# Second-stage scores over all 128 rows from copied operands, and value products only behind the first stage's groups

## The chip, the cores and the metric

The kernel runs on one core of one Trainium2 chip. The metric is device time in microseconds of one execution. A core has TensorE (PE: matrix products and transposes through the PE; its weight loads are PEld in the profile), VectorE (DVE), ScalarE (ACT), GpSimd (POOL) and SyncE (SP), whose queue issues nearly all DMAs here.

## The reference, cut to what matters

Two stages, one behind the other, on 8 batches of 576 rows. The first stage is attention with 8 heads of 64 in which scores below the row's maximum less `tau` are dropped; the second is causal attention by 4 experts, of which each row keeps the two with the largest gate.

```python
# first stage: q, k, v are (8, 8, 576, 64)
scores = scale * (q @ k.T)
scores = where(scores >= max(scores) - tau, scores, -1e9)
attn = softmax(scores)
x = (attn @ v) with the heads side by side        # (8, 576, 512)

# second stage
w = softmax over the top 2 of x @ w_gate          # w_gate is (512, 4)
for e in range(4):
    q, k, v = x @ wq[e], x @ wk[e], x @ wv[e]     # 64 columns each
    a = softmax(causal(scale * (q @ k.T)))
    out += w[e] * (a @ v @ wo[e])                 # wo[e] is (64, 512)
```

## The kernel before, in words

Numbers are split in two parts where the product needs it: a high part in the rounded fp32 type (`F32R`, one pass of PE) and the rest, the low part. A product of q and k is then hi·hi + hi·lo + lo·hi; the constant `HHL` lists these three.

**First stage.** A pair `n` of heads (4 pairs a batch, 32 in all) is worked on in five steps, one for each tile of rows (`TS`: the tail tile of 64 rows first, then four of 128). `prep` transposes q and k of the next pair, splits them into `hl`, and DMAs on SP's queue copy the parts into `qt` and `kt` so that the high and the low part lie above each other in 128 rows: two products then do what three did. `scores` does the scores, maximum, threshold, exponential and scaling of one tile; `transp` transposes the probabilities of the tile two steps earlier (`LAG_T`) into buffers `pt`; `attnv` multiplies them with the values, three tiles at the fifth step and two at the second step of the next pair.

**Second stage.** When a batch has all its heads, `begin` lists three pieces of filling work: the projections of q and k for experts 0 and 1 (`q0`: ep = 0), the values and gates of all experts (`v`), and the projections for experts 2 and 3 (`q1`). `project` writes a tile `q2` (and one for k) whose rows 0 to 63 are one expert and rows 64 to 127 the other, high and low part beside each other in the free dimension. `scores2` makes the scores of one tile of rows `t` for both experts of a pair: for the four 128-row tiles there are six products over 64 rows each (three of `HHL`, two experts, alternating between the upper and the lower half of the array), and a mask product for each expert. The width is (t + 1) · 128 columns, as keys beyond the tile are masked. The tail tile, t = 4, has its own form, over 128 rows, from `q2ds`. Then `scale2` (sum, gate weight), `transp2`, `attnv2` and `output` follow.

**The order.** The order on PE is written out by hand as a plan: `queued` (line 152) adds up a plan clock `pe[1]` from a price for each instruction and 190 ns for each change of the weights' shape. Lists hold what may come next: `proj`, `S2` (tiles to be scored), `T2` (scored, to be transposed, each with an earliest plan time), `A2` (transposed, to be multiplied with the values) and `O2` (outputs). Inside a step, `fill` takes filling work until a goal, and `tiled`, called in the second to fifth step of a pair (at s = 1 and 4 behind a group of `attnv`, at s = 2 and 3 without one), does up to two value tiles and then scores one tile. After the last pair, a loop of its own works off the last batch. `pr` sets the priority by which the scheduler of the language orders instructions on each engine, SP's queue included.

Of the kernel before, what the change touches and what calls it, by code (L numbers as in the profile page):

```python
# [29 lines left out]
BETWEEN_S2, AFTER_V_END = 2000, 5000  # L30
# [9 lines left out]
T_END = (2, 3, 4, 1, 0)  # L40
# [15 lines left out]
PPB = 4  # L56
# [3 lines left out]
VB = 3  # L60
# [4 lines left out]
def kernel(  # L65
# [112 lines left out]
    def load_pair(n):  # L178
        b, hp = divmod(n, NPAIR)
        hs = slice(2 * hp, 2 * hp + 2)  # L180
        vm = one.tile([P, 2, R, D], F32, tag="vm", name=f"vm_{n}", bufs=VB)
        pr("ld")
        def load(dst, src):
            r = nc.sync.dma_start(dst, src)
            if n in (1, 2):
                tc.add_manual_dep(r.ins, SPREAD[0].name, NOSYNC, reason="order")
        for t, x in ((km, k), (qm, q)):
            load(t[:, :, :R], x[b, hs, :SM, :].rearrange("h (p r) d -> p h r d", r=R))
            load(t[:ST, :, R], x[b, hs, SM:, :].rearrange("h s d -> s h d"))
        load(vm, v[b, hs, :SM, :].rearrange("h (p r) d -> p h r d", r=R))  # L190
        for j, rows in enumerate((slice(0, ST), slice(ST, P))):
            load(vtz[n % VB][rows, j], v[b, 2 * hp + j, SM:, :])
        VS[n] = (vm, vtz[n % VB])

# [247 lines left out]
    q2ds = [zeros(f"q2d{i}") for i in range(2)]  # L442
    Q2, V2, GW, GT = {}, {}, {}, {}

    def project(b, ep, cs):

        first, last = cs[0] == 0, cs[-1] == NC - 1
        for i, (wh, wl) in enumerate(((wqh, wql), (wkh, wkl))):
            if last:
                Q2[b, ep, i] = one.tile([P, 2, S], F32R, tag=f"q2{ep}{i}", name=f"q2_{b}_{ep}_{i}")  # L450
# [89 lines left out]
    def scores2(b, t, ep):  # L540
        q2, k2 = Q2[b, ep, 0], Q2[b, ep, 1]
# [3 lines left out]
        if t < R:  # L545
            w = (t + 1) * P
# [5 lines left out]
            for i, (x, y) in enumerate(HHL):  # L552
                for j in range(2):
                    sl = slice(j * D, (j + 1) * D)
                    matmul(gg[j][:, :w], q2[sl, x, t * P:w], k2[sl, y, :w], start=(i == 0), stop=False)
            for j in range(2):
                matmul(gg[j][:, t * P:w], ident_b, mask, start=False, stop=True)
            views = [g[:, :w] for g in gg]
        else:
            w = S  # L560
            g = ps_s.tile([P, 2, 512], F32, tag="s", name=f"s2_{b}_{t}_{ep}")
            for hf in range(2):
                cols = slice(hf * HS, (hf + 1) * HS)
                for i, (x, y) in enumerate(HHL):
                    matmul(g[:, hf, :HS], q2ds[ep][:, x], k2[:, y, cols],
                                     start=(i == 0), stop=(hf == 0 and i == 2))
# [108 lines left out]
    def project_some():  # L675

        while proj:
            b, what, g = proj[0]
            if what == "v" and left.get(b - 1, 0) or any(x[1] == b - 1 and what == f"q{x[3]}" for x in S2):
                return False  # L680
            try:
# [4 lines left out]
                if what[0] == "q":  # L686
                    S2.extend((0, b, t, int(what[1])) for t in (T_MID if b < B - 1 else T_END))
                elif what == "v":
# [4 lines left out]

    def score_tile():
        _, b, t, ep = S2.pop(0)
        scores2(b, t, ep)
        if b in GW and not unscaled:
# [14 lines left out]
    def transposable():  # L712
        return due(T2) and len(unscaled) < len(T2) and len(A2) < 2
# [20 lines left out]
    def tiled():  # L734

        for _ in range(2):
            if due(A2):
                value_tile()
        if S2 and S2[0][2] < R and len(T2) < P2B:
            score_tile()  # L740
# [12 lines left out]
    load_pair(1)  # L753
    pre = iter(())
    goal = 0.0
    for i in range(N + 2):
# [24 lines left out]
        if slot:  # L781
            m, at = (n, 4) if s == 4 else (n - 1, 6)
            if 0 <= m < NPR:
                attnv(m, TS[slice(*AV_AT[at])])
                if at == 6 and m % NPAIR == NPAIR - 1:
                    begin(m // NPAIR)
            tiled()
        else:
            next(tr, None)
            if s in MORE:  # L790
                tiled()
# [10 lines left out]
        if S2 and S2[0][2] == R and len(T2) < P2B:  # L802
# [4 lines left out]
    while proj or S2 or T2 or A2 or O2:  # L807
# [9 lines left out]
        elif S2 and len(T2) < (P2B if S2[0][1] < B - 1 else PPB) and pe[1] >= since:  # L817
# [34 lines left out]
```

## Time and profile before

| what | number |
|---|---|
| median of 3 runs | 1035.93 us (1033.07 to 1035.97) |
| the profiled execution | 1033.38 us, span 1031.7 us |
| PE busy | 966.5 us, 94% of the span |
| DVE, ACT, POOL busy | 816.5, 651.6, 408.4 us |
| chain that ended last | PE 59%, DVE 17%, ACT 13%, issue 5%, POOL 4% |
| SP's queue, moved bytes | 83296 packets, 93.83 MB, 34.5% of 16 engines |

How to read it: a busy PE is not PE at its peak, because products are pipelined and overlap in the records; the distance from one start to the next says more. The chain is followed back from the last instruction, at each step to what released it. In rows of the timeline the columns are the start, the time to the end of the row's last instruction (us), the engine, the line of the code, the operation, the tiles as out<-in, the shape (rows * columns of the array, then the result), the number of instructions, and in brackets the idle time before it with what ended it. Line 159 is that of every matrix product and line 162 that of every transpose, since helpers issue them; tiles tell them apart. In rows of windows: the stretch, its length, and for each engine its busy time and its instructions, then the granted clock, the share of the DMA engines, and GB/s.

### The profile page before, as it was taken

How to read it: one execution, taken by the hardware profiler on the slowest of the kernel's cores; microseconds unless marked ns; L12 is line 12 of the kernel's file. 1: busy time of each engine (PE TensorE's matmuls, PEld its weight loads, DVE VectorE, ACT ScalarE, POOL GpSimd, SP SyncE). 2: the span in 40 equal slices, each digit the busy share in tenths (PEclk: the TensorE clock that was granted, in tenths of full speed). 3: DMA queues.
4: the chain of work that ended last, by engine and by line, in shares of the span. 5: the costliest groups of instructions: out<-in, count | busy, mean ns of one | idle time of the engine just before them, and what ended most of it. 6: DMA issues, size and time to landing. Idle time of an engine off the chain costs nothing.

```text
span 1031.7 us, 26572 instructions
## 1 busy us (share of the span) xinstructions
PE 966.5 (94%) x9520; PEld 863.5 (84%) x9520; DVE 816.5 (79%) x2374; ACT 651.6 (63%) x1564; POOL 408.4 (40%) x700
## 2 busy tenths in 40 slices
PE   4778999999999999999999999999999999999998
PEld 3676898789888898888987898978988889888975
DVE  4778688877888779888789878887788877988564
ACT  3667566765667656765667656676566765676554
POOL 2556424533244334443344332453324533433122
PEclk9998999999999999999999999999999999999999
DMA  6555423344223443225343242334322344311101
GB/s 156 142 128 141 121 73 91 102 117 119 59 72 95 133 112 93 61 68 143 90 103 94 72 124 75 91 102 126 110 56 73 96 132 112 79 30 44 42 2 46
DMA packets 83891, 96.11 MB, mean 93 GB/s; under 512 B 29745, under 2 KB 54321, under 8 KB 83761
## 3 DMA queue, kind: packets, MB, share of 16 engines
q1 hardware_dynamic: 83296, 93.83, 34.5%
q8 instruction: 76, 1.25, 0.5%
q10 hardware_dynamic: 464, 0.59, 0.2%
q14 instruction: 55, 0.44, 0.1%
HBM read 30.42 MB, written 9.44 MB: 39 GB/s over the span
## 4 chain that ended last, share of the span: by engine, by line
PE 59%; DVE 17%; ACT 13%; issue 5%; POOL 4%; DMA 1%; SPq 0%; DVEq 0%; ACTq 0%; POOLq 0%
PE av L159 18%; PE s L159 13%; PE tm L162 8%; PE pj L159 7%; DVE pp L356 5%; PE v L159 4%; PE o L159 4%; ACT p L575 3%; ACT pp L354 3%; PE t L162 3%; DVE nmx L349 3%; DVE x L439 2%; ACT pt L144 2%; PE qkT L162 2%; POOL pp L364 2%
## 5 line engine op out<-in xcount | busy, mean ns | idle before, releaser
L364 POOL TENSOR_SCALAR pp<-pp,ss 128x576 f32<-128x576 f32 x288 | 212.8, 750 | 408.4 <-DVE ss L370 313.0
L356 DVE SCALAR_TENSOR_TENSOR pp<-s,thr,pp 128x576 f32<-128x576 f32 x288 | 233.0, 814 | 77.3 <-ACT pp L354 72.5
L354 ACT ACTIVATE pp<-s,nmx 128x576 f32<-128x576 f32 x288 | 213.7, 746 | 80.6 <-DVE nmx L349 76.8
L349 DVE TENSOR_REDUCE nmx<-s 128x1 f32<-128x576 f32 x288 | 215.8, 751 | 41.6 <-PE s L159 40.4
L159 PE MATMUL s<-kt,qt 128*128 128x288 f32 x1024 | 205.3, 319 | 5.8 <-DMA qt<-hl 5.4
L162 PE MATMUL tm<-ident,pp 128*128 128x128 f32 x1152 | 166.2, 278 | 22.1 <-POOL pp L364 15.8
L159 PE MATMUL av<-pt,vm 128*64 128x128 f32 (+1 forms) x2560 | 167.8, 267 | 0.0
L159 PEld LDWEIGHTS s<-kt,qt 128*128 128x128 f32 x1024 | 151.9, 194 | 15.5 <-DMA qt<-hl 5.7
L162 PEld LDWEIGHTS tm<-ident,pp 128*128 128x128 f32 x1152 | 136.1, 143 | 33.2 <-POOL pp L364 22.6
L159 PEld LDWEIGHTS av<-pt,vm 128*64 128x64 f32 x2560 | 140.0, 138 | 15.4 <-issue 11.4
L144 ACT COPY pt<-tm 128x512 f32<-128x512 f32 x199 | 113.6, 589 | 58.6 <-PE tm L162 56.3
L575 ACT ACTIVATE p<-s,nm 128x384 f32<-128x384 f32 (+3 forms) x144 | 78.9, 551 | 63.4 <-DVE nm L573 59.0
L589 POOL TENSOR_SCALAR p<-p,sm,gw 128x512 f32<-128x512 f32 (+3 forms) x128 | 77.1, 610 | 81.4 <-ACT pt L144 35.4
L140 ACT ACTIVATE x<-av 128x256 fp32r<-128x256 f32 (+1 forms) x96 | 48.0, 500 | 71.5 <-PE av L159 49.6
L573 DVE TENSOR_REDUCE nm<-s 128x1 f32<-128x384 f32 (+3 forms) x144 | 71.1, 513 | 24.2 <-PE s L159 21.4
L162 PE MATMUL t<-ident,p 128*128 128x128 f32 x384 | 61.1, 284 | 15.9 <-DVE ss L369 8.9
L159 PE MATMUL av<-ptt,vtz 128*64 128x128 f32 (+1 forms) x640 | 68.8, 263 | 0.0
L140 ACT ACTIVATE pt<-t 128x512 f32<-128x512 f32 (+2 forms) x112 | 57.9, 541 | 15.6 <-PE t L162 14.2
L159 PE MATMUL v<-wvh,x 128*128 128x260 f32 x320 | 64.8, 287 | 0.0
L162 PEld LDWEIGHTS t<-ident,p 128*128 128x128 f32 x384 | 43.0, 144 | 25.9 <-POOL p L589 14.3
L439 DVE TENSOR_TENSOR x<-av,x 128x256 fp32r<-128x256 f32 (+1 forms) x96 | 47.6, 495 | 19.2 <-ACT x L140 16.0
L159 PE MATMUL av<-pt,v 128*64 128x128 f32 (+1 forms) x896 | 57.9, 262 | 1.9 <-ACT p L575 1.2
(132 smaller groups left out, 1808.9 us busy)
## 6 DMA issues: line engine op xcount, KB each, us to landing
kt<-hl SPq DMA_DIRECT2D x252, 144.0 KB, 2.7
qt<-hl SPq DMA_DIRECT2D x128, 128.0 KB, 2.4
km<-in_k_dram SPq DMA_DIRECT2D x32, 256.0 KB, 3.0
qm<-in_q_dram SPq DMA_DIRECT2D x32, 256.0 KB, 3.2
vm<-in_v_dram SPq DMA_DIRECT2D x32, 256.0 KB, 2.8
out_dram<-ob SPq DMA_DIRECT2D x32, 256.0 KB, 2.4
km<-in_k_dram SPq DMA_DIRECT2D x32, 32.0 KB, 2.7
qm<-in_q_dram SPq DMA_DIRECT2D x32, 32.0 KB, 2.7
```

Source lines behind the costliest of these rows:

```text
L140: nc.scalar.activation(dst, src, AF.Copy)
L144: nc.any.tensor_copy(dst, src)
L159: queued(nc.tensor.matmul(out, x, y, **kw), x, ns if x.shape[0] == P else ns / 2)
L162: queued(nc.tensor.transpose(out, x, ident), x, 109)
L349: nc.vector.tensor_reduce(nmx[:, js], sv, axis=AX.XY, op=ALU.max, negate=True)
L354: nc.scalar.activation(e, sv, AF.Exp, bias=nmx[:, js])
L356: nc.vector.scalar_tensor_tensor(e, sv, thr[:, js], e, op0=ALU.is_ge, op1=ALU.mult, accum_out=ss[:, js])
L364: nc.gpsimd.tensor_scalar(p, p, ss[:, h:h + 1], 0.0, op0=ALU.mult, op1=ALU.add)
L439: nc.vector.tensor_tensor(xl, gs, xh.bitcast(F32), op=ALU.subtract)
L573: nc.vector.tensor_reduce(nmx[:, j:j + 1], sv, axis=AX.X if t < R else AX.XY, op=ALU.max, negate=True)
L575: nc.scalar.activation(p2[:, j * SM:j * SM + w] if t < R else halves(p2[:, :S]), sv, AF.Exp, bias=nmx[:, j:j + 1], accum_out=sm[:, j:j + 1])
L589: nc.gpsimd.tensor_scalar(p, p, sm[:, j:j + 1], gg[:, j:j + 1], op0=ALU.mult, op1=ALU.mult)
```

## The change

- `scores2` multiplies over all 128 rows for the tiles of 128 rows. New tiles `q2x` (high part of q above its low part, one for each expert) and `k2x` (for each expert, the high part of k twice, one above the other, and the low part in the same way) hold the operands, so that two products a tile and expert do the work of three (and add lo·lo). The two products of an expert are followed by its mask.
- `spread2` fills them by twelve DMAs on SP's queue for each batch and pair of experts. There is one set of buffers, which every pair of experts overwrites; the last pair of experts of the last batch uses free first-stage buffers. `spread_next` issues the copies when the next tile to be scored belongs to another pair of experts, and the first tile that reads them is scored 6000 ns of plan clock later at the earliest (`AFTER_SPREAD`); the tail tile doesn't wait.
- The q2 tiles of both pairs of experts share buffers. A projection starts only when the copies of the pair before it have been issued and its tail tile has been scored.
- `tiled` takes the number of value tiles: three behind `attnv`, none at the other two steps. Up to three transposed tiles may wait (`len(A2) < 3`).
- The loads of the first stage's values leave `load_pair` for `load_values`, with two buffers instead of three, one pair ahead, behind the `attnv` of the second step.
- In the last batch the tail tile is scored first (`T_END`).

```diff
-BETWEEN_S2, AFTER_V_END = 2000, 5000
+BETWEEN_S2, AFTER_V_END, AFTER_SPREAD = 2000, 5000, 6000
-T_END = (2, 3, 4, 1, 0)
+T_END = (4, 2, 3, 1, 0)
-VB = 3
+VB = 2
...
+    def load_values(n):
+        b, hp = divmod(n, NPAIR)
+        vm = one.tile([P, 2, R, D], F32, tag="vm", name=f"vm_{n}", bufs=VB)
+        pr("ld")
...
+        load(vm, v[b, 2 * hp:2 * hp + 2, :SM, :].rearrange("h (p r) d -> p h r d", r=R))
...
+    X2 = (const.tile([P, 2, SM], F32R, name="q2x"), const.tile([P, 2, 2, SM], F32R, name="k2x"))
...
+    def spread2(b, ep):
+        qs, ks = Q2[b, ep, 0], Q2[b, ep, 1]
+        heads = [slice(j * D, (j + 1) * D) for j in range(2)]
+
+        q2x, k2x = X2 if (b, ep) != (B - 1, EP - 1) else (
+            two.tile([P, 2, SM], F32R, tag="qt", name="q2x_end"),
+            two.tile([P, 2, 2, S], F32R, tag="kt", name="k2x_end")[:, :, :, :SM])
+        Q2[b, ep] = (q2x, k2x)
+        pr("dm2")
+        for j, sl in enumerate(heads):
+            for x, rows in enumerate(heads):
+                for dst, src in ((q2x[rows, j], qs[sl, x, :SM]), (k2x[heads[0], j, x], ks[sl, x, :SM]),
+                                 (k2x[heads[1], j, x], ks[sl, x, :SM])):
+                    nc.sync.dma_start(dst.bitcast(F32), src.bitcast(F32))
...
-                Q2[b, ep, i] = one.tile([P, 2, S], F32R, tag=f"q2{ep}{i}", name=f"q2_{b}_{ep}_{i}")
+                Q2[b, ep, i] = one.tile([P, 2, S], F32R, tag=f"q2{i}", name=f"q2_{b}_{ep}_{i}")
...
-            for i, (x, y) in enumerate(HHL):
-                for j in range(2):
-                    sl = slice(j * D, (j + 1) * D)
-                    matmul(gg[j][:, :w], q2[sl, x, t * P:w], k2[sl, y, :w], start=(i == 0), stop=False)
             for j in range(2):
+                for i in range(2):
+                    matmul(gg[j][:, :w], q2x[:, j, t * P:w], k2x[:, j, i, :w], start=(i == 0), stop=False)
                 matmul(gg[j][:, t * P:w], ident_b, mask, start=False, stop=True)
...
-            if what == "v" and left.get(b - 1, 0) or any(x[1] == b - 1 and what == f"q{x[3]}" for x in S2):
+            if what == "v" and left.get(b - 1, 0) or what[0] == "q" and any(x[2] == R or (x[1], x[3]) != spread[0] for x in S2):
                 return False
...
+    def spread_next():
+
+        if S2:
+            key = (S2[0][1], S2[0][3])
+            if key != spread[0]:
+                spread2(*key)
+                spread[:] = key, pe[1] + AFTER_SPREAD
+
+    def scorable(tail):
+        return S2 and (S2[0][2] == R) == tail and (tail or pe[1] >= spread[1])
...
-        return due(T2) and len(unscaled) < len(T2) and len(A2) < 2
+        return due(T2) and len(unscaled) < len(T2) and len(A2) < 3
...
-    def tiled():
-
-        for _ in range(2):
+    def tiled(most):
+
+        for _ in range(most):
             if due(A2):
                 value_tile()
-        if S2 and S2[0][2] < R and len(T2) < P2B:
+        if scorable(False) and len(T2) < P2B:
             score_tile()
...
+            if s == 1 and n + 1 < NPR:
+                load_values(n + 1)
...
-            tiled()
+            tiled(3)
...
-                tiled()
+                tiled(0)
```

More of the change, by code (lines that the diff above doesn't have):

```diff
@@ L180, in load_pair @@
         hs = slice(2 * hp, 2 * hp + 2)
-        vm = one.tile([P, 2, R, D], F32, tag="vm", name=f"vm_{n}", bufs=VB)
         pr("ld")
@@ L189, in load_pair, with load @@
             load(t[:ST, :, R], x[b, hs, SM:, :].rearrange("h s d -> s h d"))
-        load(vm, v[b, hs, :SM, :].rearrange("h (p r) d -> p h r d", r=R))
+    def load_values(n):
+        b, hp = divmod(n, NPAIR)
+        vm = one.tile([P, 2, R, D], F32, tag="vm", name=f"vm_{n}", bufs=VB)
+        pr("ld")
+        def load(dst, src):
+            r = nc.sync.dma_start(dst, src)
+            if n < 2:
+                tc.add_manual_dep(r.ins, SPREAD[0].name, NOSYNC, reason="order")
+        load(vm, v[b, 2 * hp:2 * hp + 2, :SM, :].rearrange("h (p r) d -> p h r d", r=R))
         for j, rows in enumerate((slice(0, ST), slice(ST, P))):
@@ L540, in scores2 @@
     def scores2(b, t, ep):
-        q2, k2 = Q2[b, ep, 0], Q2[b, ep, 1]
         nmx = small.tile([P, 2], F32, tag="nmx", name=f"nm2_{b}_{ep}_{t}")
@@ L545, in scores2 @@
         if t < R:
+            q2x, k2x = Q2[b, ep]
             w = (t + 1) * P
@@ L564, in scores2 @@
                 for i, (x, y) in enumerate(HHL):
-                    matmul(g[:, hf, :HS], q2ds[ep][:, x], k2[:, y, cols],
+                    matmul(g[:, hf, :HS], q2ds[ep][:, x], Q2[b, ep, 1][:, y, cols],
                                      start=(i == 0), stop=(hf == 0 and i == 2))
@@ L687, in project_some @@
                     S2.extend((0, b, t, int(what[1])) for t in (T_MID if b < B - 1 else T_END))
+                    spread_next()
                 elif what == "v":
@@ L692, in project_some @@
         return False
+    spread = [None, 0.0]
+    def spread_next():
[6 more added lines that the diff above has]
+        return S2 and (S2[0][2] == R) == tail and (tail or pe[1] >= spread[1])
     def score_tile():
@@ L696, in score_tile @@
         scores2(b, t, ep)
+        spread_next()
         if b in GW and not unscaled:
@@ L753 @@
     load_pair(1)
+    load_values(0)
     pre = iter(())
@@ L784 @@
                 attnv(m, TS[slice(*AV_AT[at])])
+            if s == 1 and n + 1 < NPR:
+                load_values(n + 1)
+            if 0 <= m < NPR:
                 if at == 6 and m % NPAIR == NPAIR - 1:
                     begin(m // NPAIR)
-            tiled()
+            tiled(3)
         else:
@@ L801 @@
         fill(goal)
-        if S2 and S2[0][2] == R and len(T2) < P2B:
+        if scorable(True) and len(T2) < P2B:
             score_tile()
@@ L816 @@
             transpose_tile()
-        elif S2 and len(T2) < (P2B if S2[0][1] < B - 1 else PPB) and pe[1] >= since:
+        elif S2 and scorable(S2[0][2] == R) and len(T2) < (P2B if S2[0][1] < B - 1 else PPB) and pe[1] >= since:
             score_tile()
```

2 rows, old and new, of the table PR are left out of this document.

## The prediction

> **What bounds the kernel now.** I read the page first (busy shares, then the chain that ended last), next the windows of one batch in the steady part, and then the timeline of TensorE (PE) and of the SP queue in that batch.
>
> ```profile
> PE 966.5 (94%) x9520; PEld 863.5 (84%) x9520; DVE 816.5 (79%) x2374; ACT 651.6 (63%) x1564; POOL 408.4 (40%) x700
> ...
> PE 59%; DVE 17%; ACT 13%; issue 5%; POOL 4%; DMA 1%; SPq 0%; DVEq 0%; ACTq 0%; POOLq 0%
> ...
> qt<-hl SPq DMA_DIRECT2D x128, 128.0 KB, 2.4
> ```
>
> ```profile
> 310.00:432.50 122.50, 118.65 (x1198) 106.70 (x1196) 101.27 (x295) 79.65 (x193) 48.78 (x81) 1.00 0.36 96
> ```
>
> ```profile
> 432.00:442.00 10.00, 9.15 (x72) 7.00 (x72) 9.73 (x29) 7.78 (x20) 5.96 (x11) 1.00 0.69 182
> ```
>
> A batch takes 122.5 us; PE is busy for 118.65 of them at the full clock (1.00), VectorE (DVE) for 101.27. The chain is PE for 59% only: PE work that goes away shortens the run where PE stands on the chain, and gives nothing where the softmax of the second stage makes DVE the bound (9.73 of 10 us from 432 on). So I price the freed PE time first and then take 0.6 of it.
>
> **Score products.** Second-stage score tiles (s<-q,q) of one batch, PE's timeline; a tile's length is from its start to that of its mask row:
>
> ```profile
> 432.81 0.97 PE L159 MATMUL s<-q,q 64*128 64x512 f32 x6
> 433.70 0.28 PE L159 MATMUL s<-mask,ident_b 128*128 128x128 bf16 x2
> ...
> 438.54 1.21 PE L159 MATMUL s<-q,q 64*128 64x384 f32 x6
> 439.68 0.28 PE L159 MATMUL s<-mask,ident_b 128*128 128x128 bf16 x2
> ...
> 447.08 0.61 PE L159 MATMUL s<-q,q 64*128 64x256 f32 x3
> ...
> 448.51 0.28 PE L159 MATMUL s<-mask,ident_b 128*128 128x128 bf16 x2
> ...
> 450.16 0.40 PE L159 MATMUL o<-wol,zh 128*128 128x512 f32 x1
> 450.40 0.39 PE L159 MATMUL o<-woh,zl 128*128 128x512 f32 x1
> ...
> 458.80 0.55 PE L159 MATMUL s<-q,q 64*128 64x128 f32 x6
> 459.28 0.28 PE L159 MATMUL s<-mask,ident_b 128*128 128x128 bf16 x2
> ```
>
> ```profile
> 393.67 0.39 PE L159 MATMUL av<-ptt,vtz 128*64 128x128 f32 x4
> 393.89 1.04 PE L159 MATMUL av<-pt,vm 128*64 128x128 f32 x16
> 394.76 0.39 PE L159 MATMUL av<-ptt,vtz 128*64 128x128 f32 x4
> 395.08 0.80 PE L159 MATMUL s<-q,q 64*128 64x384 f32 x6
> 395.81 0.29 PE L159 MATMUL s<-mask,ident_b 128*128 128x128 bf16 x2
> ```
>
> ```profile
> 418.37 0.81 PE L159 MATMUL s<-q,q 64*128 64x256 f32 x6
> 419.12 0.28 PE L159 MATMUL s<-mask,ident_b 128*128 128x128 bf16 x2
> ```
>
> ```profile
> 426.52 0.55 PE L159 MATMUL s<-q,q 64*128 64x128 f32 x6
> 427.01 0.28 PE L159 MATMUL s<-mask,ident_b 128*128 128x128 bf16 x2
> ```
>
> ```profile
> 508.00 0.96 PE L159 MATMUL s<-q,q 64*128 64x512 f32 x6
> 508.90 0.28 PE L159 MATMUL s<-mask,ident_b 128*128 128x128 bf16 x2
> ```
>
> For one pair of experts: 0.89 + 1.14 + 1.43 + 0.48 = 3.94 us; for the other: 0.90 + 0.73 + 0.75 + 0.49 = 2.87 us; 6.8 us a batch. Afterwards a tile has four products over all 128 rows. A 128-row product with 512 columns takes 0.24 us (450.16 to 450.40), so by columns 0.94, 0.70 and 0.47 us for the three wide tiles. No row shows such a product at 128 columns: by columns four cost 0.24 us; from above today's tile of 0.49 bounds them; I take 0.35, the middle. That is 2.46 us, 4.9 a batch: 1.9 us less. The masks stay two a tile.
>
> The Trainium skill speaks against this part: "TensorEngine Tiling (Array Packing)", Tiling Modes, lists 2x row tiling as two independent 64-row tiles, and under Overview a speedup of up to 2x for a small contraction. Six 64-row products would cost three full ones, 0.71 us at 512 columns by the product above; the trace has 0.89 and 0.90. What that gives for the time is the last rival.
>
> **Groups of products with the values.** Four av products take 0.22 us when the same shape follows (393.67 to 393.89) and 0.32 when another does (394.76 to 395.08): a change of shape costs 0.10 us.
>
> ```profile
> 437.95 0.66 PE L159 MATMUL av<-pt,v 128*64 128x128 f32 x8 [0.18 <-ACT p L575]
> ```
>
> ```profile
> 554.40 0.88 PE L159 MATMUL av<-pt,v 128*64 128x128 f32 x12
> ```
>
> These are the first and last of four groups between 432.8 and 555 that hold second-stage value products alone. With `tiled(0)` behind the other steps they join the first stage's groups: eight changes less, 0.8 us a batch. The score tiles' change back to 128 rows lies inside the 6.8 us already. Holding three tiles (`len(A2) < 3`) delays outputs by one slot and can take one transposed-tile buffer more than before; the next batch's values need the last of them, and they come 20 us later:
>
> ```profile
> 475.91 0.48 PE L159 MATMUL av<-pt,v 128*64 128x128 f32 x3
> ```
>
> ```profile
> 496.34 1.45 PE v L159 x12
> ```
>
> So I cost it at nothing; if that cover is gone, transposes wait for a value product, about the 0.66 us of the first row.
>
> **The copies.** Twelve DMAs for each batch and pair of experts, 128 KB each, as the qt copies. SP's queue around the place where the first set becomes ready, with the last writer of k's low part and the first use of the new qt:
>
> ```profile
> 492.24 5.35 SPq L282 DMA_DIRECT2D kt<-hl  x8
> 497.68 2.48 SPq L282 DMA_DIRECT2D qt<-hl  x4
> 500.20 1.27 SPq L184 DMA_DIRECT2D km<-in_k_dram  x2
> 501.58 1.23 SPq L184 DMA_DIRECT2D qm<-in_q_dram  x2
> ```
>
> ```profile
> 495.42 0.46 DVE L474 TENSOR_TENSOR q<-pj,q 128x288 fp32r<-128x288 f32 x1 [0.59 <-ACT q L140]
> ```
>
> ```profile
> 512.26 0.76 PE L159 MATMUL s<-kt,qt 128*128 128x288 f32 x4
> ```
>
> A copy costs 0.62 to 0.67 us of issue: twelve take 7.8 us, and the last lands 2.4 later, 10.2 us after the first is issued; head 0 has its six after 6.3. First set: q and k are ready at 495.9, the kt copies hold the queue to 497.6, so the last lands at 507.8, and the tile that needs it stood at 508.00. The qt copies behind them would land at 510.4, before 512.26. In the other order, qt and the loads first, the last lands at 513.0: 4.5 us late, as head 1 starts half a microsecond into the tile. Second set: it overwrites the first, so it starts when the 128-column tile (427.01) has read it, about 427.2, and lands at 437.4. Summing the kernel's own prices (line 158) over the rows from there, the next slot comes 3.7 us of plan clock later, under the 6.0 of `AFTER_SPREAD`, and the one after it 8.5 later; that is the slot at 437.95. So the tile moves by one slot and finds its copies in place, or up to about 1.5 us late when PE runs ahead. I take 0.2 us of waiting at each of the 14 places (bounds 0 and 4.5): 2.8 us.
>
> Added traffic is 3.1 MB a batch beside the 11.8 of that window (96 GB/s): nothing, as the engines are busy for 0.36. The shared q2 buffers cost nothing while the copies end before the next projection, which stands behind the values in the list.
>
> **Loads of the values.**
>
> ```profile
> SPq L184 <- PE av L159: 241.5, 29, 15.2
> ```
>
> The values' loads wait at the head of SP's queue for the buffer that the first stage's products release, up to 15.2 us, and everything later waits behind. With two buffers they are issued one step after that release, with the same lead to their first use (a pair and a half, over 40 us). Nothing; where a load still waits, it would hold the new copies too, which the bound of 4.5 us covers. At the start, the loads of v leave the queue ahead of the first copies, but those waited for data: nothing.
>
> **The end.** The last batch runs alone.
>
> ```profile
> 985.00:1000.00 15.00, 12.84 (x92) 10.61 (x91) 11.95 (x45) 6.04 (x17) 4.63 (x8) 0.91 0.01 2
> ```
>
> ```profile
> 985.82 0.45 DVE L474 TENSOR_TENSOR q<-part,q 128x288 fp32r<-128x288 f32 x1
> ```
>
> ```profile
> 997.92 3.18 PE L162 MATMUL t<-ident,p 128*128 128x128 f32 x14 [2.17 <-POOL p L589]
> ```
>
> PE is idle for 2.2 of these 15 us already. Its first score tiles came right behind the projection; now they wait for copies that start at 986.3 and land at 996.5. The tail tile (now first), the rest of the values and the second projection fill some 7.5 us of that. From a score to the transposes is at least 2.6 us (maximum, exponential, sum, scaling), so transposes start near 999 instead of 997.92. The second set has buffers of its own and needn't wait. I take +2 us; the bounds are 0 and +10, the whole shift of the tiles.
>
> **Sum.** (1.9 + 0.8) x 7 batches = 18.9 us of PE time; 0.6 of it is 11.3. Less 2.8 of waits and 2 at the end: 6.5 us. The profiled execution took 1033.38 us (span 1031.7), 2.5 under the median of the three runs; 1033.38 - 6.5 is 1026.9, and as runs lie 0 to 2.6 above that execution I say 1028.
>
> **Rivals.**
> 1. All the freed PE time counts and no copy is late: 1033.4 - 18.9 + 2 = 1016.5. For it: PE is busy for 118.65 of 122.5 us. Against: DVE's 9.73 of 10 where two of the eight score tiles are.
> 2. Freed time turns into waits for DVE and ScalarE, which have the same work: gain 5, waits and end take it back; 1031 to 1036. For it: 41% of the chain is not PE, and it lies where these tiles are.
> 3. Slower: the copies queue behind qt and the loads. PE takes its instructions in order, so behind a waiting score tile stand the first stage's scores and transposes, and DVE and ScalarE behind those. At 4.5 us for each first set and 1.5 for each second, 7 x 6 = 42 us; less 11.3, plus 2: 1066; at half of that 1045. It decides from 0.6 us a place, where it eats the whole gain. For it: the queue's margin is 0.2 us in the better order. Against: the first use can move behind other work where the order of the program allows it.
> 4. Slower: 64-row pairs really cost three product times, and the excess in the rows is waiting that stays. Then each tile grows by one product: 0.235 x (512 + 384 + 256 + 128)/512 = 0.59 us a pair of experts, 9.4 over 16; less 0.8 x 7 = 5.6; plus 4.8 for copies and end: 1042. Against: 0.89 and 0.90 us for 512 columns at two different places of the batch, so the excess belongs to the pairs.
>
> **Chances.** My forecast (1021 to 1031) 0.47; rival 1 0.13; rival 2 0.19; rival 3 0.15; rival 4 0.06. A change under 0.3% (3.1 us) can't be told from none here. Faster by more: forecast and rival 1 without the forecast's upper edge, 0.58; slower: rivals 3 and 4, 0.21; the same: 0.21. The range runs from rival 1 without the loss at the end and with the last batch's own 2.7 us (1033.4 - 21.6) to rival 4 and the near part of rival 3: 1012 to 1044.
>
> **What would show it.** Score tiles over 128 rows of about 0.94, 0.70, 0.47 and 0.35 us; no group of value products alone; 24 new copies a batch with SP busy for 16 us more; PE's idle time before score tiles put down to a DMA under 0.5 us each (right) or over 2 (rival 3); batches near 121.2 us instead of 122.4 (8.5 us less over seven); PE waiting for a DMA in the last batch. Wrong it would be if the batch doesn't shorten, or if the end grows by over 5 us.

## The result, and the profile after

The changed kernel took 1018.76 us (median of 4 runs, 1016.23 to 1021.54) beside 1035.68 us for the kernel before on the same chip: ratio 0.9843, interval 0.9811 to 0.9875, so 16.9 us faster, where the prediction had 8. The profiled execution took 1021.54 us (span 1019.8), the longest of the four. From the page of the kernel after: busy times, the chain that ended last, and the new copies.

```profile
PE 953.5 (93%) x9392; PEld 866.3 (85%) x9392; DVE 820.7 (80%) x2387; ACT 644.8 (63%) x1551; POOL 406.7 (40%) x699
...
q1 hardware_dynamic: 98656, 119.01, 45.6%
...
PE 69%; DVE 12%; ACT 8%; issue 4%; POOL 3%; DMA 2%; SPq 1%; DVEq 0%; POOLq 0%; ACTq 0%
...
k2x<-q SPq DMA_DIRECT2D x120, 128.0 KB, 2.4
...
q2x<-q SPq DMA_DIRECT2D x60, 128.0 KB, 2.4
```

PE's share of the chain rose from 59% to 69%, at the cost of DVE and ScalarE: PE stood less often behind the softmax. (These are 15 of the 16 sets of copies; the last writes tiles of other names.)

To find where the time went I cut each run at two marks that every version has: the first product `s<-hl,qd` of the ninth pair of heads (the third batch's first) and that of the 29th (the last batch's first). Between them lie five batches in the steady state; behind the second mark lies the time with the last batch and the end. Windows between the marks, kernel before and kernel after:

```profile
233.00:845.50 612.50, 592.74 (x5952) 532.79 (x5951) 505.83 (x1472) 397.58 (x960) 243.35 (x400) 1.00 0.36 96
845.50:1031.70 186.20, 175.25 (x1679) 154.34 (x1677) 134.49 (x397) 108.77 (x280) 59.48 (x97) 0.99 0.19 51
```

```profile
234.60:831.40 596.80, 577.46 (x5857) 529.51 (x5855) 507.45 (x1480) 393.25 (x953) 243.64 (x402) 1.00 0.49 125
831.40:1019.80 188.40, 177.92 (x1680) 159.13 (x1678) 134.96 (x401) 108.55 (x283) 58.09 (x96) 0.99 0.34 88
```

The spans differ by 11.9 us: 1.6 lost up to the first mark, 15.7 gained in five batches (122.5 us a batch became 119.4), 2.2 lost behind them. So the gain is 3.1 us for each steady batch, and the end is a small loss, near the 2 us predicted. The 1.6 us are not the change's: up to the mark the granted clock of these two executions was 0.96 and 0.93, and g2_end_two_queues below, the same program up to the last batch, came to the mark at 231.5 us with 0.96. The spans differ by less than the medians (16.9), as the profiled execution of the kernel before lay 2.3 us under its median, that of the change 2.8 over.

The mean of 119.4 hides an alternation. By the starts of `s<-hl,qd`, the five batches of the kernel before take 122.4 to 122.7 us each; those of the change take 120.5, 117.5, 120.6, 117.6 and 120.6.

The new score tiles, on PE's timeline of the kernel after:

```profile
470.72 0.44 PE L159 MATMUL s<-k2x,q2x 128*128 128x128 f32 x2
471.00 0.23 PE L159 MATMUL s<-mask,ident_b 128*128 128x128 bf16 x1
471.04 0.42 PE L159 MATMUL s<-k2x,q2x 128*128 128x128 f32 x2
471.30 0.23 PE L159 MATMUL s<-mask,ident_b 128*128 128x128 bf16 x1
...
510.60 0.73 PE L159 MATMUL s<-k2x,q2x 128*128 128x512 f32 x2
511.17 0.23 PE L159 MATMUL s<-mask,ident_b 128*128 128x128 bf16 x1
511.21 0.71 PE L159 MATMUL s<-k2x,q2x 128*128 128x512 f32 x2
511.77 0.23 PE L159 MATMUL s<-mask,ident_b 128*128 128x128 bf16 x1
...
515.62 0.62 PE L159 MATMUL s<-k2x,q2x 128*128 128x384 f32 x2 [0.29 <-ACT ptt L140]
516.08 0.23 PE L159 MATMUL s<-mask,ident_b 128*128 128x128 bf16 x1
516.12 0.60 PE L159 MATMUL s<-k2x,q2x 128*128 128x384 f32 x2
516.56 0.23 PE L159 MATMUL s<-mask,ident_b 128*128 128x128 bf16 x1
```

Measured as in the prediction, from a product's start to that of the mask behind it, the four products take 0.57 + 0.56 = 1.13 us at 512 columns, 0.46 + 0.44 = 0.90 at 384 and 0.28 + 0.26 = 0.54 at 128. The prediction had 0.94, 0.70 and 0.35; the six half-height products before took 0.89, 0.73 to 1.14 and 0.48. Each tile is 0.19 or 0.20 us over its forecast. Where the old tile was not disturbed, the new one is longer than it: by 0.24, 0.17 and 0.06 us.

### The profile page after: what moved, and what is told of

Same layout as the page of the kernel before. It is cut to its first block, busy times and chain, and to the rows that moved or that the text cites. A ratio compares the mean times of both kernels' runs of the same rounds, so it can differ in the third digit from the quotient of the medians.

```text
span 1019.8 us, 26692 instructions
## 1 busy us (share of the span) xinstructions
PE 953.5 (93%) x9392; PEld 866.3 (85%) x9392; DVE 820.7 (80%) x2387; ACT 644.8 (63%) x1551; POOL 406.7 (40%) x699
## 4 chain that ended last, share of the span: by engine, by line
PE 69%; DVE 12%; ACT 8%; issue 4%; POOL 3%; DMA 2%; SPq 1%; DVEq 0%; POOLq 0%; ACTq 0%
PE av L159 20%; PE s L159 16%; PE tm L162 9%; PE pj L159 7%; PE o L159 5%; PE v L159 4%; PE t L162 4%; DVE pp L364 3%; DVE nmx L357 3%; ACT pp L362 2%; PE qkT L162 2%; ACT p L598 2%; DVE x L447 2%; ACT x L140 1%; POOL pp L372 1%
## 5 line engine op out<-in xcount | busy, mean ns | idle before, releaser
L159 PE MATMUL av<-pt,vm 128*64 128x128 f32 (+1 forms) x2560 | 165.7, 267 | 0.0
L144 ACT COPY pt<-tm 128x512 f32<-128x512 f32 x186 | 106.7, 590 | 55.2 <-PE tm L162 54.2
L598 ACT ACTIVATE p<-s,nm 128x576 f32<-128x576 f32 (+3 forms) x144 | 78.6, 551 | 50.5 <-DVE nm L596 47.5
L596 DVE TENSOR_REDUCE nm<-s 128x1 f32<-128x576 f32 (+3 forms) x144 | 70.2, 512 | 14.5 <-PE s L159 13.0
L159 PE MATMUL s<-k2x,q2x 128*128 128x384 f32 (+3 forms) x240 | 64.3, 362 | 9.1 <-ACT ptt L140 3.6
L159 PE MATMUL av<-ptt,vtz 128*64 128x128 f32 (+1 forms) x640 | 66.2, 264 | 0.0
L359 DVE SCALAR_TENSOR_TENSOR thr<-nmx,tau_p 128x1 f32<-128x1 f32 x288 | 57.9, 204 | 2.1
```

The costliest lines, as they stand in the source:

```text
L144: nc.any.tensor_copy(dst, src)
L159: queued(nc.tensor.matmul(out, x, y, **kw), x, ns if x.shape[0] == P else ns / 2)
L596: nc.vector.tensor_reduce(nmx[:, j:j + 1], sv, axis=AX.X if t < R else AX.XY, op=ALU.max, negate=True)
L598: nc.scalar.activation(p2[:, j * SM:j * SM + w] if t < R else halves(p2[:, :S]), sv, AF.Exp, bias=nmx[:, j:j + 1], accum_out=sm[:, j:j + 1])
```

## The experiments

Medians in us; the kernel before had medians of 1032.89 to 1033.94 in these comparisons. The last three columns are from the profiled execution: the time to the mark at the ninth pair, five steady batches, and the rest. The time to the mark moves with the granted clock up to there, which was 0.93 to 0.98 in these executions, so differences of a few us in that column say nothing of an edit.

| kernel | median | ratio (95%) | to mark | five batches | rest |
|---|---|---|---|---|---|
| before (its own profile) | 1035.68 | 1 | 233.0 | 612.5 | 186.2 |
| the change | 1018.76 | 0.9843 (0.9811–0.9875) | 234.6 | 596.8 | 188.4 |
| e1_groups | 1022.62 | 0.9892 (0.9875–0.9910) | 232.0 | 598.1 | 190.2 |
| e2_scores | 1023.96 | 0.9905 (0.9888–0.9923) | 229.0 | 602.3 | 189.3 |
| e3_two_products | 1022.85 | 0.9898 (0.9879–0.9918) | 230.9 | 605.7 | 184.0 |
| e4_by_head | 1041.60 | 1.0072 (1.0045–1.0098) | 227.7 | 602.7 | 204.2 |
| e5_later_values | 1017.22 | 0.9835 (0.9809–0.9862) | 231.7 | 592.7 | 190.8 |
| e6_values_between | 1029.62 | 0.9956 (0.9938–0.9973) | 226.8 | 605.0 | 194.3 |
| e7_no_copies | 1004.45 | 0.9709 (0.9680–0.9738) | 231.4 | 589.2 | 185.3 |
| e8_loads | 1033.40 | 0.9989 (0.9973–1.0004) | 230.3 | 612.1 | 186.5 |
| f1_values_1200 | 1038.32 | 1.0052 (1.0035–1.0069) | 236.8 | 613.5 | 190.8 |
| f2_transposes_later | 1027.31 | 0.9933 (0.9907–0.9959) | 230.2 | 601.9 | 194.3 |
| f3_spread_9000 | 1015.79 | 0.9830 (0.9797–0.9864) | 227.9 | 595.0 | 189.6 |
| f4_values_4500 | 1033.93 | 1.0013 (0.9995–1.0031) | 230.9 | 596.6 | 206.3 |
| g1_change_2800 | 1017.04 | 0.9852 (0.9824–0.9879) | 229.8 | 593.0 | 191.6 |
| g2_end_two_queues | 1018.56 | 0.9860 (0.9833–0.9887) | 231.5 | 596.7 | 188.3 |
| g3_outputs_later | 1015.03 | 0.9826 (0.9806–0.9846) | 235.8 | 593.1 | 186.7 |
| g4_both | 1016.40 | 0.9836 (0.9808–0.9864) | 228.5 | 590.8 | 192.2 |
| h1_later_two_products | 1011.21 | 0.9784 (0.9748–0.9820) | 230.9 | 594.3 | 185.6 |
| h2_outputs_earlier | 1023.49 | 0.9904 (0.9878–0.9929) | 230.1 | 600.6 | 190.2 |

**First four: the parts of the change alone.** e1_groups is the kernel before with the value products grouped:

```diff
-            tiled()            # at s = 1, 4
+            tiled(3)
-                tiled()        # at s = 2, 3
+                tiled(0)
-        ... and len(A2) < 2
+        ... and len(A2) < 3
```

> The kernel before, with only the grouping of the change: three value tiles behind the first stage's products, none at the other two steps, three transposed tiles may wait. Scores stay on 64 rows. Theory A (PE time: every microsecond of PE work that is gone shortens the batch, and the grouping removes eight changes of shape a batch, 0.8 us): 7 x 0.8 = 5.6 us, ratio 0.995, batches 121.6 us. Theory B (the grouping is what pays, since PE and the softmax engines are no longer interrupted at the steps where scores are made): most of the 2.8 us a batch, ratio 0.981 to 0.986. Theory C (what pays is that one expert's scores are complete before the other's begin): no change, 0.997 to 1.003.

Measured: 0.9892, between what theories A and B expect, and 2.9 us less in each steady batch. Yet the changes of shape on PE only fell from 328 to 306 in the whole run, and 22 of them at 0.10 us are 2.2 us, not 11 (in a steady batch from 38 to 34, where the prediction counted eight less). The order on PE changed with the edit; what it saved is not what the edit is named for.

e2_scores is the change without that part (`tiled(2)` at all four places, `len(A2) < 2`).

> The changed kernel, with the grouping undone: two value tiles at each of the four steps, two transposed tiles may wait. Scores over 128 rows and copies stay. Theory A: it keeps what the products save, some 1.9 us a batch, and loses the 0.8 us of the grouping: ratio to the kernel before 0.989. Theory B: nearly all of the gain is gone and the end costs 7 us: 1.000 to 1.007. Theory C: it keeps the gain, 0.984 to 0.987.

Measured: 0.9905, 2.0 us less in a batch, near theory A's 0.989. The parts alone gain 1.1% and 0.95%, together 1.6%: they do not add up.

e3_two_products takes one of three products away from the old score tiles, and keeps the plan clock as it was:

```diff
-            for i, (x, y) in enumerate(HHL):
+            for i, (x, y) in enumerate(HHL[:2]):
...
+            pe[1] += w / 2.4 + 11
```

> The kernel before, with the third score product (low part of q by high part of k) left out in the 128-row tiles of the second stage; the plan clock is charged for it as before, so that the order stays. It takes 0.24, 0.18, 0.12 and 0.06 us of PE work out of the tiles, 1.2 us a batch, and nothing else. It measures which share of freed PE time the batch gives back. The forecast's 0.6: batches 121.7 us, ratio 0.995. Theory A (share 1): 121.2 us, 0.992. If PE time isn't what counts (theories B and C): under 0.3 us a batch, 0.998 or more.

Measured: 6.8 us less over five batches, 1.35 a batch, for about 1.2 us of product time taken out. On an order near that of the kernel before (its four pairs of heads take 31.0, 32.2, 28.1 and 29.9 us, where before's take 31.2, 32.6, 29.4 and 29.2, so it is not the very same), freed PE time came back in full, not for 0.6 of it.

e4_by_head issues the old products expert by expert, each followed by its mask, so that neighbours no longer use opposite halves of the array.

```diff
-            for i, (x, y) in enumerate(HHL):
-                for j in range(2):
-                    ... matmul(gg[j][:, :w], q2[sl, x, ...], k2[sl, y, :w], ...)
             for j in range(2):
+                for i, (x, y) in enumerate(HHL):
+                    matmul(gg[j][:, :w], q2[sl, x, ...], k2[sl, y, :w], ...)
                 matmul(gg[j][:, t * P:w], ident_b, mask, ...)
```

> The kernel before, with the six 64-row products ordered as in the change: three of one expert, its mask, three of the other, its mask. The pairs no longer run side by side, so PE work rises (three products more a tile, up to 0.59 us for two pairs of tiles, 1.8 us a batch at the 0.24 us of 512 columns and less by columns). Theory A: slower by up to 7 x 1.8 = 12 us, 1.008 to 1.012. Theory B: the same or slower. Theory C (one expert's maximum and exponential begin half a tile earlier): faster in spite of it, 0.99 or less.

Measured: 1.0072, near theory A's figure, but not by its way, as the stages show. PE's timeline of e4_by_head, one tile of 512 columns:

```profile
506.04 0.96 PE L159 MATMUL s<-q,q 64*128 64x512 f32 x3
506.94 0.23 PE L159 MATMUL s<-mask,ident_b 128*128 128x128 bf16 x1
507.10 0.96 PE L159 MATMUL s<-q,q 64*128 64x512 f32 x3
507.99 0.23 PE L159 MATMUL s<-mask,ident_b 128*128 128x128 bf16 x1
```

Three products take 0.90 us here, as long as six did in alternation (432.81 to 433.70 before). So the halves did work side by side. How well, the starts inside that old tile show, pair by pair (three narrow windows of the kernel before):

```profile
432.81 0.50 PE L159 MATMUL s<-q,q 64*128 64x512 f32 x2
...
433.14 0.40 PE L159 MATMUL s<-q,q 64*128 64x512 f32 x2
...
433.37 0.40 PE L159 MATMUL s<-q,q 64*128 64x512 f32 x2
```

The middle pair, with its own kind on both sides, takes 0.23 us, no more than one product over 128 rows (0.24); the pairs at the two ends, each beside another shape, take 0.33. So a pair costs one full product, as rival 4 has it, and the excess of 0.19 us over three of them stands at the two changes of shape. It is not the waiting that rival 4 names; nor does it belong to the pairs as such, which was the prediction's argument against that rival.

The other surprise is larger: by the rows of this tile (0.90 us more) and of the one with 128 columns (0.48 more) a batch holds several microseconds of added PE work (an estimate), and still the five steady batches were 9.8 us shorter than before's. The loss is all in the rest, 18 us. More work, shorter batch: the order on PE matters more here than the work.

**The order by itself.** The plan decides by due times when a transposed or scored tile may go. e5_later_values is the kernel before with one of these constants moved, and no work added or removed:

```diff
-AFTER_S2, AFTER_V, AFTER_T2, AFTER_AV2 = 7000, 8500, 1800, 2000
+AFTER_S2, AFTER_V, AFTER_T2, AFTER_AV2 = 7000, 8500, 2800, 2000
```

> The kernel before, with one constant of the plan changed: a transposed tile waits 2800 ns of plan clock for its value products instead of 1800. No work is added or removed. Theory A (freed PE time and nothing else): no change, 0.998 to 1.002. Theory B (grouping as such): no change. Theory D (the order before repeats an unlucky set of waits of about 3 us each batch, and any other order loses them): faster by several us, 0.990 to 0.996, batches near 120.5 us instead of 122.4.

Measured: 0.9835, as much as the whole change, and more than even theory D expected. Windows between the marks, e5_later_values:

```profile
231.70:824.40 592.70, 582.46 (x5927) 528.09 (x5925) 506.35 (x1483) 388.09 (x944) 244.02 (x402) 1.00 0.38 99
824.40:1015.20 190.80, 182.24 (x1713) 159.75 (x1711) 134.76 (x402) 108.97 (x283) 57.48 (x95) 0.98 0.19 52
```

A steady batch takes 118.5 us with all the old score products in it. One of before's waits can be followed. PE, GpSimd, DVE and, over the five batches, PE's waits in the kernel before:

```profile
411.94 0.63 PE L162 MATMUL t<-ident,p 128*128 128x128 f32 x4 [1.28 <-DVE ss L369]
412.41 0.27 PE L162 MATMUL t2t<-ident,p 128*128 128x128 f32 x1
```

```profile
408.21 2.17 POOL L589 TENSOR_SCALAR p<-p,sm,gw 128x512 f32<-128x512 f32 x3
410.35 0.83 POOL L589 TENSOR_SCALAR p<-p,sm,gt 128x576 f32<-128x576 f32 x1
411.16 0.67 POOL L589 TENSOR_SCALAR p<-p,sm,gw 128x384 f32<-128x384 f32 x1
```

```profile
411.34 0.45 DVE L474 TENSOR_TENSOR q<-pj,q 128x288 fp32r<-128x288 f32 x1
411.71 0.16 DVE L369 TENSOR_SCALAR ss<-ss 128x2 f32<-128x2 f32 x1
```

```profile
PE t L162 <- DVE ss L369: 6.4, 5, 1.3
PE pj L159 <- ACT ptt L140: 2.9, 5, 0.6
```

The row names `ss`, the update of DVE that came last; the transposes don't read it. Nor is GpSimd the cause, though its last scaling ends at 411.83: these are the tail tile's transposes (four and `t2t`), and the tail tile's own `p`, of 576 columns, was scaled by 411.18. What fits is `q<-pj,q`, the low part of a projection, which ends at 411.79: at all seven places of the run that have this wait the transposes start 0.135 us behind its semaphore update, while their distance from GpSimd's varies between 0.096 and 0.106. The program gives a reason, argued and not shown: transposes and projections take their PSUM buffers from the same four (`gbank`), and `q<-pj,q` is the last to read one. The "5" says that the same wait stood in each of the five batches. In e5_later_values, the transposes `t` have no wait for GpSimd's `p` or for `ss` in these five batches; the largest is another, and smaller:

```profile
PE t L162 <- DVE hl L269: 5.2, 9, 0.9
PE s L159 <- ACT pt L144: 1.8, 5, 0.4
```

e6_values_between moves the value products of e1_groups to the other steps: `tiled(0)` behind `attnv`, `tiled(3)` at s = 2 and 3.

> The kernel before, with value tiles at the opposite steps: up to three at the two steps without first-stage products, none behind these products; three transposed tiles may wait. Each run of value tiles stands alone between other shapes, so there are more changes of shape than in the grouping. Theory B (grouped value products): slower than the grouping alone (0.989), near 1.000 or above. Theory D (any other order): again 0.987 to 0.995.

Measured: 0.9956, just outside what theory D expects; a batch is 1.5 us shorter though the value products now stand apart from the first stage's. The rest is 8 us longer.

e7_no_copies is the change without its copies: `q2x` and `k2x` are cleared once, so that the scores of the 128-row tiles in the second stage are not those of the inputs.

> The changed kernel without its copies: the score products of the 128-row tiles read operands that stay zero, so these scores are left out; all products and the plan's waiting time remain. The forecast charged the copies 2.8 us in the steady part and 2 at the end. If the copies hide (their waits in the profile of the change are 0.4 us in single places): gain over the change 0 to 2 us in the batches, and at the end up to the 9 us by which the copies stand on the chain of waits there: ratio to the kernel before 0.975 to 0.984. If the queue slows the first stage: batches shorter than 117 us, ratio under 0.97.

Measured: 0.9709, between its two cases, and 13.9 us below the change by the spans (3.2 up to the mark, where the granted clocks differ too; 7.6 in five batches; 3.1 in the rest). Windows of e7_no_copies:

```profile
231.40:820.60 589.20, 574.84 (x5856) 528.85 (x5855) 505.94 (x1485) 391.18 (x948) 243.93 (x402) 1.00 0.38 100
```

So the copies, hidden as they look, cost about 1.5 us a batch on average. But the cost does not lie in every batch: without copies the five take 117.6, 117.5, 118.3, 117.5 and 118.4 us, so the change's first, third and fifth lose 2.2 to 2.9 us, and its second and fourth lose nothing. The order on PE differs here too, so that these are the copies with whatever their absence does to the order.

e8_loads is the kernel before with `load_values` and `VB = 2` alone.

> The kernel before, with only the loads of the first stage's values moved behind the products of the second step, and two buffers instead of three. The forecast: nothing, 0.998 to 1.002. If the values' loads at the head of SP's queue delay the first stage's copies today: faster, 0.997 or less.

Measured: 0.9989, no difference, as predicted.

**More constants.** f1_values_1200 and f4_values_4500 set the same constant to 1200 and 4500 in the kernel before, f2_transposes_later sets `AFTER_S2` to 8000; f3_spread_9000 is the change with `AFTER_SPREAD = 9000`.

> The kernel before, with 1200 instead of 1800 ns of plan clock between a transposed tile and its value products. 2800 took 16.7 us off. Theory M (value products that stand too close behind the copy of their transposed tile on ScalarE make PE wait, and all behind them): earlier is no better than before, 1.000 or slower. Theory D (any other order loses an unlucky set of waits): faster again, 0.983 to 0.995.

> The kernel before, with 4500 instead of 1800 ns of plan clock between a transposed tile and its value products. Theory M: about what 2800 gave, 0.982 to 0.988, as the wait is gone at either distance. Theory D: faster by an amount that isn't foreseen, and not tied to the distance.

> The kernel before, with 8000 instead of 7000 ns of plan clock between a score tile and its transposes; the distance from the transposes to the value products stays at 1800. Theory M: the same distance, so little change, 0.996 to 1.003. Theory D: faster, 0.983 to 0.995.

> The changed kernel, with 9000 instead of 6000 ns of plan clock between the issue of the copies and the first tile that reads them. Without copies every batch takes 117.5 to 118.3 us; with them every second one takes 120.6, and in those the second set lands at 565.7 while the first tile that needs it stands at 562.1. If lateness is the cost: no batch over 118.5 us, 1.5 us a batch less, ratio to the kernel before 0.970 to 0.976. If the copies cost by filling SP's queue or the engines: no gain, 0.984.

Measured: f1 1.0052, with batches of 122.7 us as before's; theory D, in which any other order is faster, falls with it. f4 has batches of 119.3 us, 3.2 shorter, and loses it all in the rest (206.3): 1.0013, against theory M. f2 0.9933, as theory D expects and M does not. f3 0.9830, no difference from the change that its interval can tell, and its mean batch is 119.0 us beside 119.4. What f3 took away were late sets of copies. In the kernel after, SP's queue and PE at one such place:

```profile
555.85 0.54 SPq L468 DMA_DIRECT2D q2x<-q  x1
...
562.65 1.24 SPq L468 DMA_DIRECT2D k2x<-q  x2
```

```profile
562.12 0.50 PE L159 MATMUL s<-k2x,q2x 128*128 128x512 f32 x1
...
564.55 0.47 PE L159 MATMUL s<-k2x,q2x 128*128 128x512 f32 x1 [0.24 <-DMA q2x<-q]
```

The second set is still being issued when the tile starts; it lands at 565.7, 3.6 us behind that start. First-stage work fills part of the gap and PE waits for a DMA for 0.24 us only, but the tile's fourth product comes at 567.61, where it comes 0.93 us behind the first in a tile that is not disturbed. In the five batches four of the ten sets land after their tile's first product: two in the first batch, one in the third, one in the fifth. These are the batches of 120.5 and 120.6 us; the two without a late set take 117.5 and 117.6. In f3 no set of these batches is late and none takes 120.6, but its other order gives 119.3 or 119.4 us to each batch from the second on. So f3's equal mean does not clear lateness. g1 and g4 below speak for it: g1 has late sets in its first batch alone, which takes 120.5 us, and 117.5 to 118.4 in the others; g4 has none, and 117.5 to 118.4 in all. Against it: e2, whose order is another again, has late sets in all five and takes 119.0 to 122.3. No run changes the lateness and nothing else.

**Does it add?** g1_change_2800 is the change with e5's constant. g2_end_two_queues is the change with the low parts' copies of the last batch on ScalarE's queue. g3_outputs_later is the kernel before with `AFTER_AV2 = 3000` in place of 2000. g4_both is the change with `AFTER_T2 = 2800`, `AFTER_SPREAD = 9000` and g2's queue.

> The changed kernel, with 2800 instead of 1800 ns of plan clock between a transposed tile and its value products; in the kernel before this one constant took 16.7 us off without any change of work. If the change's 17 us are the same waits gone (theory D): the two do not add, ratio to the kernel before 0.980 to 0.988. If they are work that is gone (theory A): they add, 0.965 to 0.972.

> The changed kernel, with half of the copies of the last batch (those of the low parts) issued by ScalarE's queue. Twelve copies on one queue take 7.8 us, and stand on the chain of waits at the end for some 9 us; without any copies the end was 3 us shorter. If the issue is what costs there: 2 to 3 us less than the change, ratio 0.981 to 0.983. If the projections or ScalarE set the end: no change, 0.984 to 0.986.

> The kernel before, with 3000 instead of 2000 ns of plan clock between the last value products of a tile and its output products: an order change that leaves the distance of value products from their transposes alone. Theory D: batches of 118 to 121 us instead of 122.4 and a ratio under 0.995. Theory M (only the distance of the value products counts): 122 us or more, 0.998 to 1.003.

> The changed kernel with three settings at once: 2800 ns ahead of the value products, 9000 ns behind the copies, the last batch's copies on two queues. If the gains add: 3 us for the end and up to 1 us a batch, 0.974 to 0.980. If the batches stand at their floor of 117.5 to 119 us by now: only the end, 0.980 to 0.983.

Measured: g1 0.9852 and g4 0.9836: on top of the change the constant gives nothing that can be told from none, so the two gains don't add. That they are the same waits does not follow. In the rows of windows PE is idle (length less busy time) for 19.8 us of the five batches before and 19.3 in the change, but for 10.2 in e5 and 9.6 in g3: the change shortened the time in which PE's records show it busy, e5 and g3 both. A floor that the better orders share, near 117.5 to 119 us a batch, would also keep gains from adding; no run separates the two. g2 0.9860: nothing, so taking half of these copies off SP's queue does not shorten the end. g3 0.9826, a second constant, of another list, with the same gain:

```profile
235.80:828.90 593.10, 583.54 (x5940) 529.04 (x5938) 509.17 (x1491) 385.66 (x932) 243.16 (x400) 1.00 0.37 99
```

h1_later_two_products is g3 with e3's cut, and h2_outputs_earlier the kernel before with `AFTER_AV2 = 1000`.

> The kernel before with 3000 ns ahead of the output products (17.9 us faster than the kernel before, batches of 118.6 us), and without the third score product of the 128-row tiles, the plan charged for it as before. On the old order the same cut took 10.9 us and 1.25 us a batch. If freed PE time counts on the better order too: another 8 to 11 us, batches near 117.4 us, ratio to the kernel before 0.972 to 0.975. If the better order has reached the floor of the other engines: 0.980 to 0.984.

> The kernel before, with 1000 instead of 2000 ns of plan clock ahead of the output products. Every change of order that gained so far came later (values 2800, outputs 3000, transposes 8000); values earlier (1200) did not gain. Theory D (any other order): faster, under 0.995, batches of 118 to 121 us. Theory E (second-stage work stands too early and too close in the order before): no gain, 0.998 or more, batches of 122 us or more.

Measured: h1 0.9784, between its two cases. On g3's order the same cut of 1.2 us a batch gave nothing in the five batches (594.3 beside 593.1); what h1 is below g3, 0.4% with overlapping intervals, lies outside them. h2 0.9904: moving the constant the other way gains too. A theory by which only later slots gain falls with it; f1 is the only order tried that kept before's batch, and nearly every other order lost 1.5 to 4 us of it.

No version beats the change by more than the intervals allow among those that compute all of the reference: g3 and f3 are level with it. h1, and e7 even more, leave work out.

## Why the prediction was right or wrong

The time lay in the range, and the sign was right, but the sum was not: the gain was double the one forecast. The step that failed is the sum: it freed 2.7 us of PE time a batch, of which the runs show about 1.4, and had no term for what another order does to the time between all other instructions, where about 1.7 came from.

- **The order (missing).** The sum treated the place of each instruction as given and took 0.6 of the freed time. In this kernel an edit of prices or due times can give another order on PE, and before's order held waits that came back in every batch. e5 and g3 remove no work and gain 1.65% and 1.74%; the change gains 1.57% and does not add to e5's. Put down, from start to start on PE over the five batches, to the instruction that a stretch begins with, the 3.1 us a batch divide so: 0.4 in the score products, 1.0 in the products with the values of both stages, 1.7 in all others, which have the same work in both kernels. This is an estimate, as a wait is put down to the instruction ahead of it. It does not say that the 1.7 us are the waits that e5 loses: PE's idle time is nearly that of before, so they lie in instructions that follow each other more closely. The chain of 59% PE was read as a discount on freed work. It was also the sign of time to be had without freeing any.
- **Score products, 1.9 us a batch (mis-sized).** All tiles of the five batches together take 6.4 us a batch beside 6.8: 0.4 us less. The sum also took the old tiles of 1.14 and 1.43 us for work. Their kind takes 0.72 undisturbed at 384 columns, and at 256 columns 0.55 in g3, so part of the old 6.8 was disturbance. Against undisturbed tiles the new ones are longer by the growth that rival 4 gives. Two things were left out of their price. The new price had columns only, but the first product still comes behind another shape: 0.57 us for two where 0.47 were counted, the 0.10 that the prediction itself had read. The Trainium skill, "TensorEngine Tiling (Array Packing)", Key Properties, says that switching the tiling mode drains TensorE; the trace agrees with 0.10 us each. And the masks now stand between the two experts, where before both came last: the pair behind a bf16 mask (511.21 to 511.77) takes 0.56 us, 0.09 over.
- **Changes of shape, 0.8 us a batch.** More went than the eight counted, 18 (38 became 20); some of their price lies in the tiles. The products with the values are 1.0 us a batch shorter, near this term. e1 shows how little the grouping alone removed, four changes a batch.
- **The share of 0.6 (not confirmed).** e3 gave more than 1, h1 gave 0 in the batches. Whether freed PE time counts depends on the order it is freed in.
- **The copies, 2.8 us of waits (too small).** Part of the row-by-row reading held: twelve take 8 us, a tile moves, PE's wait for a DMA is 0.24 us. But four of ten sets landed 2.3 to 4.1 us behind the start of their tile, three of them second sets, for which the prediction allowed 1.5. By e7 the batches with them lost 7.6 us together. The prediction counted only PE's direct waits, and by its own sign for this, idle time put down to a DMA, the copies look harmless.
- **The end, +2.** Measured +2.2, and the copies stand where they were expected to. The size may be luck: the same column moves by up to 20 us with the order, and issuing half of these copies on another queue (g2) took nothing off. From the chain of waits of the kernel after, the copies stand on it, eight issues from 972.26 on (first and last), and then the landing:

```profile
972.26 0.47 SPq L468
...
976.64 0.60 SPq L468
977.24 0.04 issue
977.28 4.13 DMA k2x<-q
```

- **Held as predicted:** the loads cost nothing (e8), batches got shorter (119.4 us, where 121.2 were expected), DVE's work is unchanged (505.8 and 507.5 us in five batches).
- **Rivals.** Rival 1 named nearly the time that came (1016.5), by luck: freed work was about 1.4 us a batch, not 2.7, and copies were late. Rival 2 had the right suspicion, that freed time need not count, but PE's idle time did not grow (19.8 and 19.3 us in five batches). Rival 3's late copies did happen, in the batches of 120.6 us, at 2.2 to 2.9 us a batch instead of the 6 that it needs. Rival 4 had the price of the old tiles right (0.23 us for a pair) and with it the growth of the new ones, but not its reason, and not the time, since the other instructions drew together by more than the tiles grew.

What stays open: which first shift makes before's order so slow; the followed wait is 1.3 us of a batch, and the change still has as much idle time on PE as before. Further, whether late copies alone make the three slow batches of the change, since e7, f3, g1 and g4 change the order as well. And the split of the change's own gain: better order (as in e5 or g3), freed work (e7 is 1.2% below g3) and copies (about 1.3%) would make up its 1.6%, but no run holds the order fixed.

## What to carry to other kernels

Before a gain is credited to the work an edit removes, move one or two due times of the plan that remove nothing; where these gain as much, the gain can't be credited to the work by its size alone: compare PE's busy and idle time too. Cut every run at the same marks and compare the steady period and the end apart, because here each constant moved both, often against each other. Check for each copy whether it landed ahead of the product that reads it, batch by batch: other work that fills the gap hides the wait from a list of waits, and a mean hides that only every second batch is slow. Price a new group of products with its neighbours: the shape ahead of it and the type of what stands in the middle.

## What the runs showed of the hardware

A product of rounded fp32 behind a bf16 product costs about 0.09 us more than behind one of its own kind (0.56 us for two of 512 columns, where 0.47 were counted). Two 64-row products of 512 columns in opposite halves take 0.23 us together when their own kind stands on both sides, as one product over 128 rows does (0.24), and 0.10 more beside a change of shape. Three 64-row products in the same half take 0.90 us, and six that alternate between the halves 0.89. The same instructions in another order, on an engine that is 94% busy by its records, ran from 1.7% faster to 0.5% slower, and the time behind the second mark differed by up to 20 us (186.2 and 206.3).
